# Low passes of the product with v, and tile 0's scores, threaded between the transposes of their slot

## The chip, the cores and the metric

The kernel runs on one core of a Trainium2 chip. The time is the device time of one execution in microseconds (us). TensorE (PE) multiplies; loading its weights is listed by itself as PEld. VectorE is DVE, ScalarE is ACT, GpSimd is POOL, and SP is the engine that issues most transfers. PSUM is the memory TensorE writes to; the kernel uses six banks of it in rotation (tag `b`) and two as accumulators.

## The reference

Attention with a forgetting gate, then a layer norm and a two-layer network with a residual:

```python
scores = scale * q @ k.T                        # 8 batches x 8 heads, 576 tokens, 64 wide
decay = cum[:, None] - cum[None, :]             # cum = cumsum(log(clip(f, 1e-4, 1)))
scores = where(causal, -1e9, scores + decay)
attn = softmax(scores);  x = attn @ v           # heads side by side: 8 x 576 x 512
xn = (x - mean) / sqrt(var + 1e-6) * g_ln
out = x + relu(xn @ w_ch1) @ w_ch2              # 512 -> 2048 -> 512
```

All values are f32. To multiply exactly enough at the faster fp32r rate, most operands are split into a high part (rounded to fp32r) and a low part (the residual), and a product is the sum of high x high, high x low and low x high passes.

## The kernel before

**Slots.** The 64 heads are cut into query tiles: tile 0 has the first 64 queries, tiles 1 to 4 have 128 each (`QT`, line 296). Tile t sees the keys up to its own: 64, 192, 320, 448 and 576. The loop at line 811 runs over slots (head, t) with t = 1 to 4; slot t = 1 also does tile 0. With `LAG` = 2, a slot computes the scores of its own tile, transposes the softmaxed tile of two slots ago, and, if the slot three ago was t = 2 or 4, does the product with v for that pair of tiles. So in the steady state of a head:

| slot | scores | product with v | transposes (64-column block, 128-column blocks) |
|---|---|---|---|
| t = 1 | tiles 0 and 1 | tiles 0 to 2 of the head before | tile 3 of the head before: 1, 3 |
| t = 2 | tile 2 | none | tile 4 of the head before: 1, 4 |
| t = 3 | tile 3 | tiles 3, 4 of the head before | tiles 0 and 1: 2, 1 |
| t = 4 | tile 4, in two halves | none | tile 2: 1, 2 |

Every slot from number 35 on also carries one step of the network (`mm1`, lines 624 to 626, 12 matmuls of 256 columns; `mm2`, lines 646 to 648, 6 matmuls of 512 columns of the step before). 64 such steps remain behind the last slot.

**Two kinds of head.** The first 16 heads (`NFULL`) multiply in f32 and have no low passes. The other 48 split their operands: scores are `hi` x `hi` (L377) plus `kl`, `xq` (L378); the product with v (`av_unit`, line 512) has high passes with both halves of v as 128-column weights (`both(k)`, moving `ph`) and low passes with the 64-column high half of v (moving `pl`). All write the bank `o`.

**A tile's way.** `softmax_a` (DVE L410) adds the mask and scales the scores and takes the row minimum of the negated values. `softmax_e` (ACT L421) takes the exponential with its row sum. `softmax_b` (DVE L426, L427, POOL L428) normalizes; a transfer (`pw<-p`, SP) copies the tile as fp32r. Two slots later `transpose_unit` (line 455) puts its blocks through TensorE into the bank `tr` (L447; L449 for f32). A block's weights are the 64 or 128 columns of the tile, its moving operand is the identity of 128 columns. `transposed_hi` (ACT L505) rounds `tr` to `ph`, and `transposed_lo` (DVE L510) writes the residuals: for the 64-key block into the lower half of `ph`, for the others into `pl`. So both kinds of pass read what DVE wrote. `finish` (ACT L580) copies the upper half of `o` to `ot`; `finish_add` (DVE L591) adds it to the lower half and gives `xs`, which is sent to memory.

**The order** in a slot is written out by hand in `ORDERS` (line 50): one letter a piece, one string for each stage. Every engine runs its own instructions in exactly that order.

```python
(66, "QSAFteahBlMPrmNbRLD"),
```

This third string holds from slot 66 to the last, number 258. Q is the scores, S `softmax_a`, A the product with v, F `finish`, t the transposes, e the exponential, a `finish_add`, h and l the two casts, B `softmax_b`, M `mm1`, P preparations of the next head (ACT L343, L349, DVE L350, L357), r and m the split of the hidden values (ACT L632, DVE L637), N `mm2` and, after a chunk's last step, the output (DVE L723), b the statistics of rows (ACT L687, DVE L692, L693), R loads and splits of the network's input (ACT L607, DVE L609), L and D small steps and loads. A bank is taken again once its last reader in this order is through; banks are handed out in the order in which they came free.

A chunk of the network has 256 tokens and 16 steps, so the work of N, b and R beyond the single step repeats every 16 slots, that is every four heads.

Of the kernel before, what the change touches and what calls it, by code (L numbers as in the profile page):

```python
# [17 lines left out]
P = 128  # L18
# [30 lines left out]

ORDERS = [  # L50
    (0, "WwQsSthAeMrgFBmlLNPaRf"),
    (37, "WwQSstAMhPelgNFrfmBDLRba"),
    (66, "QSAFteahBlMPrmNbRLD"),
]


# [1 line left out]
def attn_moe(ctx: ExitStack, tc: tile.TileContext, qk, v, f, g, w1, w2, out):  # L58
# [396 lines left out]
    def transpose_unit(h, t):  # L455
        n = f"{h.n}"
        pt = h.p[t][0]
        work_ = []
        if t <= 2:
            if t == 1:  # L460
                if h.full:
                    h.ph1 = padded_keys("ph1", 704, S1)
                else:
                    h.ph1 = work.tile([P, 704], F32R, tag="ph1", bufs=1, name=f"ph1_{n}")
                h.pl1 = None if h.full else pools["late"].tile([P, 384], F32R, tag="pl1", bufs=1, name=f"pl1_{n}")
            ph = h.ph1
            pl = ph if h.full else h.pl1
            tp = bank(f"tr{n}_{t}")
            if t == 1:
                tr(tp[0:64, 0:128], h.p[0][0])  # L470
                tr(tp[0:64, 64:192], pt[:, 0:64])
                tr(tp[:, 192:320], pt[:, 64:192])
                work_.append((tp[0:64, 0:192], ph[0:64, 0:192], ph[64:128, 0:192]))
                work_.append((tp[:, 192:320], ph[:, 320:448], pl[:, 0:128]))
            else:
                tr(tp[0:64, 0:128], pt[:, 0:64])
                tr(tp[:, 128:256], pt[:, 64:192])
                tr(tp[:, 256:384], pt[:, 192:320])
                work_.append((tp[0:64, 0:128], ph[0:64, 192:320], ph[64:128, 192:320]))
                work_.append((tp[:, 128:384], ph[:, 448:704], pl[:, 128:384]))  # L480
        else:
            if t == 3:
                if h.full:
                    h.ph2 = padded_keys("ph2", 9 * P, S - S1)
                else:
                    h.ph2 = work.tile([P, 9 * P], F32R, tag="ph2", bufs=1, name=f"ph2_{n}")
                h.pl2 = None if h.full else pools["late"].tile([P, 7 * P], F32R, tag="pl2", bufs=1, name=f"pl2_{n}")
            c = 0 if t == 3 else P
            ph = h.ph2[:, : 8 * P].rearrange("p (k c) -> p k c", k=4)[:, :, c : c + P]
            pl = None if h.full else h.pl2[:, : 6 * P].rearrange("p (k c) -> p k c", k=3)[:, :, c : c + P]  # L490
            tp = bank(f"tr{n}_{t}").rearrange("p (k c) -> p k c", k=4)
            tr(tp[0:64, 0, :], pt[:, 0:64])
            for k in range(1, 4):
                tr(tp[:, k, :], pt[:, 64 + P * (k - 1) : 64 + P * k])
            work_.append((tp[0:64, 0, :], ph[0:64, 0, :], ph[64:128, 0, :]))
            work_.append((tp[:, 1:4, :], ph[:, 1:4, :], pl))
            if t == 4:
                tp = bank(f"tr{n}_4b")[:, :P]
                tr(tp, pt[:, 64 + 3 * P : 64 + 4 * P])
                work_.append((tp, h.ph2[:, 8 * P :], None if h.full else h.pl2[:, 6 * P :]))  # L500
        h.parts = work_

    def transposed_hi(h, t):
        for tp, hi, lo in h.parts:
# [7 lines left out]
    def av_unit(h, t):  # L512
        po = bank(f"o{h.n}_{t}")

        if h.full:

            def fac(cols, k, mv, first=False):
                half = slice(0, 64) if cols.start < SPLIT[t] else slice(64, P)
                mm(po[half, cols], h.vr[:, k], mv, start=first, stop=True, skip_group_check=True)  # L519

            if t == 2:
                ph = h.ph1
                for k, c0, q0 in ((0, 0, 0), (1, 320, 64)):
# [12 lines left out]
            return  # L536

        vv = h.vv

        def both(k):  # L540
            return vv[:, k].rearrange("p a d -> p (a d)")

        def acc(o, st, mv, first=False):
            mm(o, st, mv, start=first, stop=True, skip_group_check=True)  # L544

        if t == 2:
            ph, pl, w, c0 = h.ph1, h.pl1, S1, 0
            acc(po[:, 0:320], both(0), ph[:, 0:320], True)
            acc(po[:, 64:320], both(1), ph[:, 320:576])
            acc(po[:, 192:320], both(2), ph[:, 576:704])  # L550
            acc(po[0:64, 64:320], vv[:, 1, 0, :], pl[:, 0:256])
            acc(po[0:64, 192:320], vv[:, 2, 0, :], pl[:, 256:384])
        else:
            ph, pl, w, c0 = h.ph2, h.pl2, S - S1, S1
            for k in range(4):
                acc(po[:, 0:256], both(k), ph[:, 256 * k : 256 * k + 256], k == 0)
# [4 lines left out]
        h.o = (po, w, c0)  # L561

    xs_tile = {}

# [246 lines left out]
    for u, slot in enumerate(slots):  # L811

        def before(k):
            return slots[u - k] if u >= k else None

        if slot is not None:
            n, t = slot
            h = hd[n]
        av = None
        if before(LAG + 1) is not None and before(LAG + 1)[1] in (2, 4):  # L820
            av = hd[before(LAG + 1)[0]]
        want = moe.can(wp.ready()) and u >= FIRST_MOE

        def piece(c):
            tu = before(LAG)
            if c == "t" and tu is not None:
                transpose_unit(hd[tu[0]], tu[1])
            elif c == "h" and tu is not None:
                transposed_hi(hd[tu[0]], tu[1])
            elif c == "l" and tu is not None:  # L830
                transposed_lo(hd[tu[0]])
            elif c == "Q" and slot is not None:
                if t == 1:
                    qk_mm(h, 0)
                qk_mm(h, t)
            elif c == "A" and av is not None:
                av_unit(av, before(LAG + 1)[1])
            elif c == "S" and slot is not None:
                if t == 1:
                    softmax_a(h, 0)  # L840
                softmax_a(h, t)
            elif c == "e" and slot is not None:
                if t == 1:
                    softmax_e(h, 0)
                softmax_e(h, t)
            elif c in FILL:
                wp.fill(FILL[c])
            elif c == "s":
                wp.sums()
                if u == LAG:  # L850
                    busy(WARM[2])
            elif c == "F" and av is not None:
                finish(av)
            elif c == "a" and av is not None:
                finish_add(av)
            elif c == "r" and want:
                moe.first_high()
            elif c == "R":
                moe.limit = min(NCHUNK, max(0, u - LAG - 1) // (4 * H) * S // C)
                moe.rest()  # L860
            elif c == "b":
                rows_stats(moe.cur)
            elif c == "L":
                run_later(RSTD)
            elif c == "M" and want:
                moe.first()
            elif c == "B" and slot is not None:
                if t == 1:
                    softmax_b(h, 0)
                softmax_b(h, t)  # L870
            elif c == "m" and want:
                moe.first_low()
            elif c == "W":
                due = 1 + min(u, W_CHANGE) / W_SLOTS + max(0, u - W_CHANGE) * W_TICKS
                while not wp.done() and wp.tick_no <= due:
                    wp.tick()
            elif c == "N":
                moe.second()
            elif c == "P":
                prep()  # L880
            elif c == "D":
                next_raw()
# [90 lines left out]
```

## Time and profile before

| | |
|---|---|
| median of 3 runs | 1208.62 us (1208.13 to 1209.88) |
| the profiled execution | 1208.3 us |
| its span, first to last instruction | 1206.5 us |
| granted TensorE clock, mean | 0.997 |
| TensorE busy, span from 0 to 105 us | 91.00 us |
| TensorE busy, 250 to 990 us | 739.71 of 740 us |
| VectorE busy, 250 to 990 us | 530.23 us |
| ScalarE busy, 250 to 990 us | 411.47 us |
| GpSimd busy, 250 to 990 us | 331.25 us |

The first third of the table is the device time; the rest comes from one profiled execution. A matmul's recorded time runs from its start to the end of its pass through the array, which overlaps with the passes behind it: what a pass costs is read from the distance of two starts, not from its duration. A weight load runs beside the pass before it. An instruction of DVE or ACT is likewise listed with its whole latency, and the next may start a little before it has ended. In brackets stands the idle time of the engine before an instruction, and what ended it.

### The profile page before, as it was taken

Reading aid. Unit: us, or ns where it says so; the run is one execution under the profiler, and the core shown is the slowest. Engines: PE = TensorE matmul, PEld = TensorE weight load, DVE = VectorE, ACT = ScalarE, POOL = GpSimd, SP = SyncE. Lnnn points to the kernel's source line nnn. Section 1 sums busy time; section 2 is a strip of 40 time slices with the busy share of each in tenths; the row PEclk is TensorE's granted clock in tenths of the full one; section 3 lists DMA queues with packets and bytes.
Section 4 is the critical chain, followed back from the end, with each engine's and each line's share of the span. In section 5 each row is a group of like instructions: output and inputs, shape, how many; then the busy total and the mean of one; then the engine's idle time right before and its main releaser. Section 6 shows DMA issues by size and latency. Waiting matters only on the chain.

```text
span 1206.5 us, 25720 instructions
## 1 busy us (share of the span) xinstructions
PE 1187.0 (98%) x8368; PEld 1066.3 (88%) x8368; DVE 752.9 (62%) x2658; ACT 619.4 (51%) x1936; POOL 456.6 (38%) x774
## 2 busy tenths in 40 slices
PE   8889999999999999999999999999999999999998
PEld 6667888999999999999999999999999999999997
DVE  6787684476767777777767676767676752122222
ACT  5887575555555555555555555555565532111111
POOL 3445345344545444453545453444454410000000
PEclk9999999999999999999999999999999999999999
DMA  6455442344444443434343434444343421111100
GB/s 193 133 166 169 131 135 82 99 134 131 134 133 130 132 140 125 138 130 144 130 145 120 144 124 128 137 125 147 123 140 127 120 87 40 32 36 40 32 28 26
DMA packets 127541, 139.00 MB, mean 115 GB/s; under 512 B 32432, under 2 KB 100016, under 8 KB 127408
## 3 DMA queue, kind: packets, MB, share of 16 engines
q1 hardware_dynamic: 127408, 137.36, 37.2%
q8 instruction: 67, 1.10, 0.4%
q14 instruction: 66, 0.54, 0.2%
HBM read 79.61 MB, written 19.17 MB: 82 GB/s over the span
## 4 chain that ended last, share of the span: by engine, by line
PE 91%; DVE 3%; ACT 2%; DMA 1%; issue 1%; POOL 0%; SPq 0%; DVEq 0%; POOLq 0%; ACTq 0%
PE h L624 12%; PE h L626 11%; PE h L625 11%; PE acc L646 11%; PE acc L647 11%; PE acc L648 11%; PE o L544 6%; PE tr L447 4%; PE s L377 3%; PE s L378 3%; PE s L375 2%; PE o L519 2%; PE tr L449 1%; DVE p L410 1%; PE pc L202 1%
## 5 line engine op out<-in xcount | busy, mean ns | idle before, releaser
L428 POOL TENSOR_SCALAR p<-p,st 64x64 f32<-64x64 f32 (+4 forms) x320 | 169.6, 531 | 497.5 <-ACT ph L505 246.7
L624 PE MATMUL h<-x,w1h 128*128 128x256 f32 x1152 | 341.7, 297 | 0.4 <-DVE st L410 0.4
L626 PE MATMUL h<-x,w1l 128*128 128x256 f32 x1152 | 326.2, 283 | 0.0
L625 PE MATMUL h<-x,w1h 128*128 128x256 f32 x1152 | 325.7, 283 | 0.0
L421 ACT ACTIVATE p<-p,st 64x64 f32<-64x64 f32 (+4 forms) x320 | 179.2, 560 | 210.1 <-DVE st L410 205.7
L637 DVE SCALAR_TENSOR_TENSOR hh<-h,hh 128x256 fp32r<-128x256 f32 x288 | 120.5, 418 | 186.5 <-ACT hh L632 184.1
L646 PE MATMUL acc<-w2h,hh 128*128 128x512 f32 x576 | 228.4, 397 | 0.0
L647 PE MATMUL acc<-w2l,hh 128*128 128x512 f32 x576 | 227.8, 395 | 0.0
L648 PE MATMUL acc<-w2h,hh 128*128 128x512 f32 x576 | 225.4, 391 | 0.0
L624 PEld LDWEIGHTS h<-x,w1h 128*128 128x128 f32 x1152 | 219.0, 190 | 5.3 <-issue 0.9
L625 PEld LDWEIGHTS h<-x,w1h 128*128 128x128 f32 x1152 | 220.0, 191 | 2.4
L626 PEld LDWEIGHTS h<-x,w1l 128*128 128x128 f32 x1152 | 219.7, 191 | 0.0
L632 ACT ACTIVATE hh<-h 128x256 fp32r<-128x256 f32 x288 | 109.9, 382 | 181.2 <-PE h L626 180.7
L410 DVE CUSTOM_DVE_ANT_0 p<-s,mask 64x64 f32<-64x64 f32 (+4 forms) x320 | 132.3, 421 | 26.2 <-PE s L378 17.4
L648 PEld LDWEIGHTS acc<-w2h,hh 128*128 128x128 f32 x576 | 108.5, 188 | 24.7
L426 DVE TENSOR_SCALAR st<-st 128x1 f32<-128x1 f32 (+1 forms) x320 | 47.7, 149 | 121.3 <-ACT p L421 118.2
L646 PEld LDWEIGHTS acc<-w2h,hh 128*128 128x128 f32 x576 | 109.4, 190 | 14.0 <-issue 0.2
L647 PEld LDWEIGHTS acc<-w2l,hh 128*128 128x128 f32 x576 | 109.4, 190 | 11.7
L505 ACT CAST ph<-tr 64x128 fp32r<-64x128 f32 (+4 forms) x384 | 107.2, 328 | 3.7 <-PE tr L447 1.3
L580 ACT COPY ot<-o 64x320 f32<-64x320 f32 x96 | 38.0, 396 | 124.1 <-PE tr L447 62.6
L510 DVE TENSOR_TENSOR pl<-tr,ph 128x128 fp32r<-128x128 f32 x192 | 88.0, 458 | 4.4
L378 PE MATMUL s<-kl,xq 66*128 66x288 f32 (+4 forms) x288 | 83.3, 297 | 0.0
(90 smaller groups left out, 1886.0 us busy)
## 6 DMA issues: line engine op xcount, KB each, us to landing
raw<-in_qk_dram SPq DMA_DIRECT2D x96, 288.0 KB
wr<-in_w_dram SPq DMA_DIRECT2D x32, 512.0 KB
pw<-p SPq DMA_DIRECT2D x48, 288.0 KB
pw<-p SPq DMA_DIRECT2D x48, 224.0 KB
vr<-in_v_dram SPq DMA_DIRECT2D x64, 160.0 KB
out_dram<-xt SPq DMA_DIRECT2D x36, 256.0 KB
pw<-p SPq DMA_DIRECT2D x48, 160.0 KB
xa<-xs SPq DMA_DIRECT2D x32, 160.0 KB
```

The costliest lines, as they stand in the source:

```text
L378: mm(sp, xq, kl, start=False, stop=True)
L410: nc.vector.tensor_tensor_reduce(out=pt[:m, a:z], in0=sp, in1=mask[:m, off + a : off + z], scale=-SCALE, scalar=3.0e38 if i == 0 else st[: ...
L421: nc.scalar.activation(pt[:m, :w], pt[:m, :w], AF.Exp, bias=st[:m, i : i + 1], scale=-1.0, accum_out=st[:m, 2:3])
L428: nc.gpsimd.tensor_scalar(out=pt[:m, :w], in0=pt[:m, :w], scalar1=st[:m, 3:4], scalar2=1.0, op0=ALU.mult, op1=ALU.mult)
L624: mm(ph, w1h[:, k, fs], c.x[k][:, 0, :], start=(k == 0), stop=False)
L625: mm(ph, w1h[:, k, fs], c.x[k][:, 1, :], start=False, stop=False)
L626: mm(ph, w1l[:, k, fs], c.x[k][:, 0, :], start=False, stop=(k == KT - 1))
L632: nc.scalar.activation(h[:, 0, :], c.ph, AF.Relu)
L637: nc.vector.scalar_tensor_tensor(out=h[:, 1, :], in0=ph, scalar=0.0, in1=h[:, 0, :].bitcast(F32), op0=ALU.max, op1=ALU.subtract)
L646: mm(c.acc[i], h[:, 0, ts_], w2h[:, j, :], start=(j == 0), stop=False)
L647: mm(c.acc[i], h[:, 0, ts_], w2l[:, j, :], start=False, stop=False)
L648: mm(c.acc[i], h[:, 1, ts_], w2h[:, j, :], start=False, stop=(j == FT - 1))
```

## The change

Four things move; no matmul, cast or transfer is added or taken away.

- In every group of transposes the 64-column blocks come last.
- The low passes of the product with v are no longer issued by `av_unit`; it returns them as a list, the shortest first. The piece t (`row`) issues them: one behind each wide transpose as long as another wide one follows and more than one low pass is left, the rest at the end of the row.
- Tile 0's scores (of the heads with split operands) leave Q and are issued in the row, behind the transposes and ahead of the remaining low passes. Their `softmax_a` and `softmax_e` are the new piece z.
- In the third string F moves from behind A to behind t and e, with z behind it; in the second, z comes behind l. In B tile 1 is normalized ahead of tile 0, in all heads.

```diff
-    (37, "WwQSstAMhPelgNFrfmBDLRba"),
-    (66, "QSAFteahBlMPrmNbRLD"),
+    (37, "WwQSstAMhPelzgNFrfmBDLRba"),
+    (66, "QSAteFzahBlMPrmNbRLD"),
...
             if t == 1:
+                tr(tp[:, 192:320], pt[:, 64:192])
                 tr(tp[0:64, 0:128], h.p[0][0])
                 tr(tp[0:64, 64:192], pt[:, 0:64])
-                tr(tp[:, 192:320], pt[:, 64:192])
...
-            acc(po[0:64, 64:320], vv[:, 1, 0, :], pl[:, 0:256])
-            acc(po[0:64, 192:320], vv[:, 2, 0, :], pl[:, 256:384])
+            low = [
+                lambda: acc(po[0:64, 192:320], vv[:, 2, 0, :], pl[:, 256:384]),
+                lambda: acc(po[0:64, 64:320], vv[:, 1, 0, :], pl[:, 0:256]),
+            ]
...
-            for k in range(1, 4):
-                acc(po[0:64, 0:256], vv[:, k, 0, :], pl[:, 256 * (k - 1) : 256 * k])
-            acc(po[0:64, 128:256], vv[:, 4, 0, :], pl[:, 6 * P :])
+            low = [
+                lambda: acc(po[0:64, 128:256], vv[:, 4, 0, :], pl[:, 6 * P :]),
+                lambda: acc(po[0:64, 0:256], vv[:, 1, 0, :], pl[:, 0:256]),
+                lambda: acc(po[0:64, 0:256], vv[:, 2, 0, :], pl[:, 256:512]),
+                lambda: acc(po[0:64, 0:256], vv[:, 3, 0, :], pl[:, 512:768]),
+            ]
...
+        def row():
+            tu = before(LAG)
+            trs = [] if tu is None else transpose_unit(hd[tu[0]], tu[1])
+            wide = [x for x in trs if x[1].shape[1] > 64]
+            narrow = [x for x in trs if x[1].shape[1] <= 64]
+            while wide:
+                tr(*wide.pop(0))
+                if wide and len(lows) > 1:
+                    lows.pop(0)()
+            for x in narrow:
+                tr(*x)
+            if slot is not None and t == 1 and not h.full:
+                qk_mm(h, 0)
+            while lows:
+                lows.pop(0)()
...
             elif c == "B" and slot is not None:
-                if t == 1:
-                    softmax_b(h, 0)
-                softmax_b(h, t)
+                for i in [1, 0] if t == 1 else [t]:
+                    softmax_b(h, i)
+            elif c == "z" and slot is not None and t == 1 and not h.full:
+                softmax_a(h, 0)
+                softmax_e(h, 0)
```

So the slot t = 1 issues on TensorE: tile 1's scores, three high passes, wide transpose, low pass of 128 columns, two wide transposes, the 64-column block, tile 0's scores, low pass of 256 columns. The slot t = 3: tile 3's scores, five high passes, the wide transpose, two 64-column blocks, four low passes.

More of the change, by code (lines that the diff above doesn't have):

```diff
@@ L457, in transpose_unit, with tr @@
         pt = h.p[t][0]
-        work_ = []
+        work_, row = [], []
+        def tr(out_, in_):
+            row.append((out_, in_))
         if t <= 2:
@@ L475, in transpose_unit @@
             else:
-                tr(tp[0:64, 0:128], pt[:, 0:64])
                 tr(tp[:, 128:256], pt[:, 64:192])
                 tr(tp[:, 256:384], pt[:, 192:320])
+                tr(tp[0:64, 0:128], pt[:, 0:64])
                 work_.append((tp[0:64, 0:128], ph[0:64, 192:320], ph[64:128, 192:320]))
@@ L491, in transpose_unit @@
             tp = bank(f"tr{n}_{t}").rearrange("p (k c) -> p k c", k=4)
-            tr(tp[0:64, 0, :], pt[:, 0:64])
             for k in range(1, 4):
@@ L497, in transpose_unit @@
             if t == 4:
-                tp = bank(f"tr{n}_4b")[:, :P]
-                tr(tp, pt[:, 64 + 3 * P : 64 + 4 * P])
-                work_.append((tp, h.ph2[:, 8 * P :], None if h.full else h.pl2[:, 6 * P :]))
+                tb = bank(f"tr{n}_4b")[:, :P]
+                tr(tb, pt[:, 64 + 3 * P : 64 + 4 * P])
+                work_.append((tb, h.ph2[:, 8 * P :], None if h.full else h.pl2[:, 6 * P :]))
+            tr(tp[0:64, 0, :], pt[:, 0:64])
         h.parts = work_
+        return row
     def transposed_hi(h, t):
@@ L535, in av_unit @@
                 h.o = (po, S - S1, S1)
-            return
+            return []
         vv = h.vv
@@ L557, in av_unit @@
             acc(po[:, 128:256], both(4), ph[:, 8 * P :])
-            for k in range(1, 4):
-                acc(po[0:64, 0:256], vv[:, k, 0, :], pl[:, 256 * (k - 1) : 256 * k])
-            acc(po[0:64, 128:256], vv[:, 4, 0, :], pl[:, 6 * P :])
+            low = [
[4 more added lines that the diff above has]
+            ]
         h.o = (po, w, c0)
+        return low
     xs_tile = {}
@@ L818, in attn_moe @@
             h = hd[n]
-        av = None
+        av, lows = None, []
         if before(LAG + 1) is not None and before(LAG + 1)[1] in (2, 4):
@@ L822, in attn_moe, with tiles @@
         want = moe.can(wp.ready()) and u >= FIRST_MOE
+        def tiles(h, t):
+            return [0, 1] if t == 1 and h.full else [t]
+        def row():
[13 more added lines that the diff above has]
+                lows.pop(0)()
         def piece(c):
             tu = before(LAG)
-            if c == "t" and tu is not None:
-                transpose_unit(hd[tu[0]], tu[1])
+            if c == "t":
+                row()
             elif c == "h" and tu is not None:
@@ L832, in piece @@
             elif c == "Q" and slot is not None:
-                if t == 1:
-                    qk_mm(h, 0)
-                qk_mm(h, t)
+                for i in tiles(h, t):
+                    qk_mm(h, i)
             elif c == "A" and av is not None:
-                av_unit(av, before(LAG + 1)[1])
+                lows.extend(av_unit(av, before(LAG + 1)[1]))
             elif c == "S" and slot is not None:
-                if t == 1:
-                    softmax_a(h, 0)
-                softmax_a(h, t)
+                for i in tiles(h, t):
+                    softmax_a(h, i)
             elif c == "e" and slot is not None:
-                if t == 1:
-                    softmax_e(h, 0)
-                softmax_e(h, t)
+                for i in tiles(h, t):
+                    softmax_e(h, i)
             elif c in FILL:
```

1 line of the change is left out of this document (removed).

## The prediction

> **What bounds the kernel now.** The page comes first: the busy table, then the chain that ended last.
>
> ```profile
> span 1206.5 us, 25720 instructions
> PE 1187.0 (98%) x8368; PEld 1066.3 (88%) x8368; DVE 752.9 (62%) x2658; ACT 619.4 (51%) x1936; POOL 456.6 (38%) x774
> PE 91%; DVE 3%; ACT 2%; DMA 1%; issue 1%; POOL 0%; SPq 0%; DVEq 0%; POOLq 0%; ACTq 0%
> ```
>
> TensorE is never idle for long and holds 91% of the chain, so a microsecond taken out of its stream is a microsecond, as long as nobody comes late to it. The stream has hidden losses, though. The timeline of PE shows one head (start, duration): its first slot, its third, and the start of the next head.
>
> ```profile
> 709.72 0.22 PE L377 MATMUL s<-hi 128*64 128x128 f32 x1
> 709.84 0.30 PE L377 MATMUL s<-hi 128*128 128x192 f32 x1
> ...
> 710.09 0.51 PE L544 MATMUL o<-ph,vv 128*128 128x320 f32 x3
> 710.44 0.34 PE L544 MATMUL o<-pl,vv 128*64 128x256 f32 x2
> 710.61 0.46 PE L447 MATMUL tr<-identr,pw 128*64 128x128 f32 x4
> 710.91 0.35 PE L624 MATMUL h<-x,w1h 128*128 128x256 f32 x1
> 711.10 0.28 PE L625 MATMUL h<-x,w1h 128*128 128x256 f32 x1
> ...
> 717.39 0.37 PE L377 MATMUL s<-hi 128*128 128x448 f32 x1
> ...
> 717.80 0.70 PE L544 MATMUL o<-ph,vv 128*128 128x256 f32 x5
> 718.34 0.57 PE L544 MATMUL o<-pl,vv 128*64 128x256 f32 x4
> 718.75 0.35 PE L447 MATMUL tr<-identr,pw 128*64 128x128 f32 x3
> 718.93 0.35 PE L624 MATMUL h<-x,w1h 128*128 128x256 f32 x1
> 719.12 0.28 PE L625 MATMUL h<-x,w1h 128*128 128x256 f32 x1
> ...
> 725.47 0.22 PE L377 MATMUL s<-hi 128*64 128x128 f32 x1
> ```
>
> Read the starts. Three transposes with 128 moving columns take 718.75 to 718.93, 0.06 each; the two tile-0 scores (709.72 to 709.84) also 0.06 each. A 256-column pass, the four low passes show it (718.34 to 718.75 for three of 256 and one of 128), takes 0.12. Yet L624 behind transposes takes 0.19 (710.91 to 711.10). The first slot: four transposes and L624 take 0.49, where 4 x 0.06 + 0.12 = 0.36 would do; 0.13 lost, with three 128-column transposes. The third slot: 0.37 against 0.30; 0.07 lost, with one. So each 128-column transpose whose weights load behind a 0.06 pass loses about 0.03, and a full load (128x128, not transposing) behind one about 0.04 to 0.05.
>
> The other side is VectorE and ScalarE, which the page calls 62% and 51% busy. Both take their instructions in the order written. Their timeline in the same head, with the end of the head before:
>
> ```profile
> 702.66 0.62 DVE L410 CUSTOM_DVE_ANT_0 p<-s,mask 128x448 f32<-128x448 f32 x1
> ...
> 706.60 0.44 DVE L410 CUSTOM_DVE_ANT_0 p<-s,mask 128x288 f32<-128x288 f32 x1
> ...
> 710.06 1.02 DVE L609 TENSOR_TENSOR x<-xr,x 128x256 fp32r<-128x256 f32 x2
> 711.00 0.21 DVE L410 CUSTOM_DVE_ANT_0 p<-s,mask 64x64 f32<-64x64 f32 x1
> ...
> 711.14 0.34 DVE L410 CUSTOM_DVE_ANT_0 p<-s,mask 128x192 f32<-128x192 f32 x1
> ...
> 711.42 0.47 DVE L591 TENSOR_TENSOR xs<-o,ot 64x320 f32<-64x320 f32 x1
> ...
> 712.82 0.28 DVE L510 TENSOR_TENSOR ph<-tr,ph 64x128 fp32r<-64x128 f32 x1 [0.31 <-ACT ph L505]
> ...
> 713.92 1.40 DVE L723 SCALAR_TENSOR_TENSOR xt<-acc,rs,xt 128x512 f32<-128x512 f32 x2
> 715.24 0.48 DVE L410 CUSTOM_DVE_ANT_0 p<-s,mask 128x320 f32<-128x320 f32 x1
> ...
> 716.97 0.28 DVE L510 TENSOR_TENSOR ph<-tr,ph 64x128 fp32r<-64x128 f32 x1 [0.17 <-ACT ph L505]
> ...
> 718.33 0.61 DVE L410 CUSTOM_DVE_ANT_0 p<-s,mask 128x448 f32<-128x448 f32 x1
> ...
> 719.41 0.42 DVE L591 TENSOR_TENSOR xs<-o,ot 64x256 f32<-64x256 f32 x1 [0.46 <-ACT ot L580]
> 720.07 0.16 DVE L426 TENSOR_SCALAR st<-st 128x1 f32<-128x1 f32 x1 [0.24 <-ACT p L421]
> ...
> 722.29 0.46 DVE L410 CUSTOM_DVE_ANT_0 p<-s,mask 128x288 f32<-128x288 f32 x1
> ...
> 725.10 0.42 DVE L510 TENSOR_TENSOR pl<-tr,ph 128x256 fp32r<-128x256 f32 x1
> ```
>
> ```profile
> 711.59 0.44 ACT L421 ACTIVATE p<-p,st 128x192 f32<-128x192 f32 x1
> ...
> 712.15 0.64 ACT L505 CAST ph<-tr 64x128 fp32r<-64x128 f32 x2
> ...
> 719.00 0.37 ACT L580 COPY ot<-o 64x256 f32<-64x256 f32 x1 [1.05 <-PE tr L447]
> 719.27 0.67 ACT L421 ACTIVATE p<-p,st 128x448 f32<-128x448 f32 x1
> ...
> 720.06 0.47 ACT L505 CAST ph<-tr 64x192 fp32r<-64x192 f32 x2
> ```
>
> VectorE is 62% busy and yet often behind: the 192-column scores stand ready soon after 710, and it reaches them at 711.14; each wait in it is a link of one chain through ScalarE and back. TensorE does not notice today, because what it needs from that chain (ph and pl, for the next product with v) comes in time: pl of 725.10 ends at 725.52, and the first low pass of the next head comes 0.72 behind its slot's start (709.72 to 710.44), at 726.19.
>
> **The change on TensorE.** Passes and columns stay the same; only neighbours change. Per head of the 48 that have low passes (64 heads less NFULL = 16): slots 2 and 4 end their row with a 64-column block in place of opening it; one 128-column load fewer stands behind a 0.06 pass, 0.03 each. Slot 3: the transposes come ahead of the low passes, so L624's load stands behind a 0.12 pass and is covered; of 0.07 the 0.03 of one transpose remain, 0.05 saved. Slot 1: tile 1's full load no longer stands behind tile 0 (0.05), L624's stands behind the 256-column low pass (0.05), and the wide transposes lose 0.03 three times as before: 0.10. Together 0.10 + 0.03 + 0.05 + 0.03 = 0.20 with unrounded shares 0.198, times 48: **9.5 us less**, if every operand is in time. A 64-column load behind a transpose has no row; between nothing and the 0.03 of a wide one, I take nothing (such loads hide behind 0.06 passes in the tile-0 scores). For two of them per head the other end is 48 x 2 x 0.03 = 2.9.
>
> A rule of the Trainium skill speaks against this term. The row first, PEld being the weight loads:
>
> ```profile
> 710.87 0.19 PEld L624 LDWEIGHTS h<-x,w1h 128*128 128x128 f32 x1
> ```
>
> This load starts at 710.87 while the transposes of 710.61 run until 711.07, on the same 128 rows. The Trainium skill, page "TensorE: Matmul & The Clock Gate", section "Part 3: Packing small matmuls — row/col tiling", says that a load overlaps running matmuls only where the row groups differ. By that rule no order hides a load, and the 9.5 would be 0; by the row it stands.
>
> The first 16 heads use f32 passes and have no low passes; there only the blocks and the normalizations of tiles 0 and 1 change places. The waits of PE say what hangs on it (who, on whom, us in total, times, longest):
>
> ```profile
> PE tr L449 <- POOL p L428: 3.7, 10, 0.7
> ```
>
> These transposes need both tiles before they end, and the second of GpSimd's two multiplications ends when it did, so I take nothing. At best the 3.7 goes; as much again could come, since tile 1's exponential is the later one.
>
> **The change on VectorE and ScalarE.** This decides. In the new order the copy of o (L580) stands behind the tile's exponential on ScalarE, and the addition L591, which reads the copy, still stands ahead of the normalization on VectorE. VectorE now waits for exponential and copy in a row, and the residuals ph, pl and the next slot's scores queue behind it.
>
> Slot 3, from the start of its scores to those of slot 4 when VectorE is late: before 718.33 to 722.29, 3.96. After: scores until the exponential 0.66 (0.61 and a short read), exponential with its read 0.79 (719.27 to 720.06), copy to addition 0.41 (719.00 to 719.41), addition 0.36, then 720.07 to 722.29 is 2.22, less 0.14 of waiting for the cast that ends at 720.53. Sum 4.30.
>
> Slot 1, likewise: before 711.00 to 713.92, 2.92. After: scores of tile 1 to the exponential 0.38, exponential 0.56 (711.59 to 712.15), copy 0.46, addition 0.40, four small steps of 0.17 0.69, residuals and hh 1.10 (712.82 to 713.92). Sum 3.59. Tile 0's scores and exponential fall into the waits.
>
> Slots 2 and 4 keep their 3.09 (715.24 to 718.33) and 3.50 (722.29 to 725.79, which is 725.10 plus the 0.69 to the next scores).
>
> Now replay. Let VectorE take 702.66 as before. The next scores start at 702.66 + 4.30 = 706.96 (before 706.60), and pl ends 3.23 later (722.29 to 725.52), at 710.19. TensorE, two heads ahead by 0.20 each, starts slot 1 at 709.32; its first low pass now comes 0.66 behind the slot's start (0.72 less tile 0's 0.12, plus one transpose), at 709.98, with 0.11 for signal and load: 710.30 against 709.98. **Wait 0.3.** VectorE is free at 710.42, does the two L609 in 0.68 (part of their 1.02 is waiting that a later start swallows; 0.68 is my choice between 0.6 and the 0.94 from 710.06 to 711.00), starts slot 1 at 711.10, slot 2 at 711.10 + 3.59 + 1.32 (both L723) = 716.01, and its ph ends 2.01 later at 718.02. TensorE reaches slot 3 at 717.39 - 0.40 - 0.13 (slots 1 and 2 of this head) + 0.3 = 717.16, and its product with v, 0.41 later, at 717.57 needs that ph. **Wait 0.5**, and 0.1 more at the low pass that now comes first. Slot 3's scores 719.10, slot 4's 723.40 (1.11 late); pl ends 726.63. TensorE's next head starts 725.47 - 0.60 + 0.3 + 0.6 = 725.77, its low pass stands at 726.43, needs 726.74. **Wait 0.3.** The following head has neither L609 nor L723 ahead of its first slots and catches up. Sum 1.2 a round. How many rounds, the grouped lines of VectorE over 250 to 990 tell:
>
> ```profile
> L723 DVE SCALAR_TENSOR_TENSOR xt<-acc,rs,xt 128x512 f32<-128x512 f32 x24 | 16.8, 742 | 0.0
> ```
>
> 24 are 12 pairs, one every fourth head: 12 x 1.2 = 14.6 with the unrounded 1.22. Sum: 1208.3 (the profiled execution's own time, its span and 1.8 around it) - 9.5 + 14.6 = 1213.4. The median of the three runs is 1208.62, 0.3 above that execution; **forecast 1213.7**.
>
> **Rivals.** (1) *Faster*: VectorE's idle time swallows the later addition. For it: the brackets above show 0.2 to 0.5 of idle several times a head. Against: each is a link of the chain that I counted. It decides if the waits of a round stay under 0.6 (0.79 saved, less 0.2). With 0.2 left a round: 1208.6 - 9.5 + 2.4 = 1201.5. Chance 0.22. (2) *No change*: the waits come only around the head with L723 (0.5 and 0.3), because the head before it is in time: 1208.6 - 9.5 + 9.6 = 1208.7. Chance 0.18. (3) *The change hides no load*: each pass pays its load in whatever order, so nothing is saved, and the waits stay: 1208.6 + 14.6 = 1223. The load that runs beside the transposes from 710.87 speaks against it. Chance 0.03. (This is what the rule cited from the Trainium skill would give.) (4) The forecast, 0.57.
>
> **How the numbers follow.** The two lengthened chains are good to some 0.15 each; three of them meet in a round, so 0.45 x 12 = 5.4 either way, 1208 to 1219. Above that, rounds whose L609 waits longer, and the DMA of pw that goes out later: 1221. Below, rival 1 reaches from 1199.1 with no waits; I cut at 1201, leaving out about 1 in 10 on each side. A measurement of this kernel tells 0.2% (2.4 us) from no change. Faster 0.22, same 0.18, slower 0.60.
>
> **What would show it.** Right: in the new trace, L624 behind the row in slots 1 and 3 takes 0.12; L591 stands idle for ACT L580 longer than now; PE L544 shows waits for DVE L510, in the heads with L723 and at the start of the next. Wrong: the scores of slot 4 start as close to TensorE as now, or the product with v never waits; then the 9.5 comes out whole. If L624 still takes 0.19, the TensorE side is wrong.

## The result and the profile after

The changed kernel takes **1230.05 us** (median of 4 runs, 1228.17 to 1232.64), the kernel before 1208.84 beside it: ratio 1.0175, 95% interval 1.0158 to 1.0192. It is slower, as forecast, but by 21 us and not by 5, and outside the range. The profiled execution has a span of 1226.4 us against 1206.5. One of the ten executions of a run below, the one without the output additions, took 2271 us, and its time there is the median of the other nine.

In the changed file most lines stand lower. The ones used here, old to new: ScalarE's cast to ph L505 to L510, VectorE's residual L510 to L515, the product with v L544 to L549, the copy of o L580 to L591, the addition L591 to L602, the chunk's cast and residual L607 and L609 to L618 and L620, the MLP's first pass L624 to L635, the output addition L723 to L734. Heads are told apart by n modulo 4, since one MLP chunk takes four heads: in n%4 = 1 the first two pieces of the chunk's input are split (L618, L620), in n%4 = 2 its row statistics are taken (L703), at the turn from n%4 = 2 to 3 the other two pieces are split, and in n%4 = 3 the output additions L734 follow. The head shown in the prediction, at 709.72, is n = 47, of the kind 3.

The page of the changed kernel:

```profile
span 1226.4 us, 25577 instructions
PE 1190.1 (97%) x8368; PEld 1062.9 (87%) x8368; DVE 745.1 (61%) x2658; ACT 626.3 (51%) x1936; POOL 454.8 (37%) x774
PE 21%; ACT 1%; issue 1%; DVE 1%; POOL 1%; DMA 0%; SPq 0%; DVEq 0%; POOLq 0%; ACTq 0%
```

No engine has more work than before, and TensorE still reads 97%. The chain of waits, 91% TensorE before, holds only a quarter of the span here: the view lost the trail, so nothing is read from it. The waits of PE say more (who, on whom, us in total, times, longest):

```profile
PE o L549 <- DVE ph L515: 12.3, 33, 0.6
PE tr L449 <- POOL p L428: 6.4, 12, 1.1
PE o L549 <- POOL rs L725: 3.0, 10, 0.3
PE tr L447 <- DMA pw<-p: 1.0, 2, 0.8
```

The product with v now waits for the residuals of ph; before, that was one wait of 0.3. But the rows give 15 us where more than 20 are missing. The timeline of PE in head 47 shows why (its first slot, its third, and the start of its fourth):

```profile
719.81 0.25 PE L377 MATMUL s<-hi 128*128 128x192 f32 x1
719.90 0.28 PE L378 MATMUL s<-kl,xq 66*128 66x192 f32 x1
720.50 0.57 PE L549 MATMUL o<-ph,vv 128*128 128x320 f32 x3 [0.32 <-POOL rs L725]
720.90 0.24 PE L447 MATMUL tr<-identr,pw 128*128 128x128 f32 x1
...
721.42 0.28 PE L549 MATMUL o<-pl,vv 128*64 128x256 f32 x1
721.54 0.28 PE L635 MATMUL h<-x,w1h 128*128 128x256 f32 x1
721.65 0.28 PE L636 MATMUL h<-x,w1h 128*128 128x256 f32 x1
...
727.91 0.37 PE L377 MATMUL s<-hi 128*128 128x448 f32 x1
728.11 0.36 PE L378 MATMUL s<-kl,xq 66*128 66x448 f32 x1
728.97 0.80 PE L549 MATMUL o<-ph,vv 128*128 128x256 f32 x5 [0.50 <-DVE ph L515]
729.61 0.37 PE L447 MATMUL tr<-identr,pw 128*128 128x128 f32 x3
729.81 0.58 PE L549 MATMUL o<-pl,vv 128*64 128x128 f32 x4
730.23 0.28 PE L635 MATMUL h<-x,w1h 128*128 128x256 f32 x1
730.35 0.28 PE L636 MATMUL h<-x,w1h 128*128 128x256 f32 x1
...
733.06 0.30 PE L377 MATMUL s<-hi 128*128 128x288 f32 x1
```

First, the saving is there: L636 follows L635 by 0.11 and 0.12 in both slots, where the kernel before took 0.19. Second, the waits are larger than their brackets. From 719.90 to 720.50 there are 0.60 between two starts that otherwise lie 0.11 apart, so 0.49 are lost, and the bracket says 0.32: the record of the pass before runs on to 720.18 and covers the first part of the wait. The Trainium skill, page "Perfetto Trace Analysis", section "Tensor Engine Instruction (MATMUL, LD_WEIGHTS)", says that the end which the profile gives a TensorE instruction is computed, not observed; the rows here agree. Waits of this engine are therefore read from start to start.

So read, slot by slot (start of a slot's first full score to the next slot's; medians over the 12 heads of a kind, in us; "copy early" and the others are runs of the next section):

| slot | before | changed | load early | no output addition | copy early | copy and load early |
|---|---|---|---|---|---|---|
| 1, n%4 = 0 | 3.97 | **4.41** | 4.40 | 4.01 | 4.01 | 4.02 |
| 1, n%4 = 2 | 4.26 | **4.83** | 4.30 | 4.91 | 4.30 | 4.30 |
| 1, n%4 = 3 | 3.97 | **4.55** | 4.45 | 4.52 | 4.01 | 4.01 |
| 3, n%4 = 3 | 4.44 | **5.13** | 5.12 | 4.40 | 4.59 | 4.60 |

Without a wait the four slots of a head take 3.97 + 3.58 + 4.44 + 3.76 = 15.75 before and 4.01 + 3.54 + 4.40 + 3.62 = 15.56 (unrounded) in the changed kernel (tile 0's 0.12 has moved from in front of slot 1 into it). That is 0.19 less; unrounded and with the longer slots of n%4 = 1 and 2 it comes to 9.4 us over 48 heads. Against it, the four places lose 0.41, 0.53, 0.54 and 0.73 in each round of four heads, 2.21, times 12 rounds 26.5 us; the waits in all other slots come to 5.6, against 2.8 before. 26.5 + 2.8 - 9.4 = 19.9, and the span grew by 19.9.

Where the waits come from, on VectorE (its timeline, heads 46 to 47):

```profile
713.17 0.62 DVE L410 CUSTOM_DVE_ANT_0 p<-s,mask 128x448 f32<-128x448 f32 x1
...
715.03 0.42 DVE L602 TENSOR_TENSOR xs<-o,ot 64x256 f32<-64x256 f32 x1 [1.22 <-ACT ot L591]
...
717.59 0.44 DVE L410 CUSTOM_DVE_ANT_0 p<-s,mask 128x288 f32<-128x288 f32 x1
...
720.06 0.28 DVE L515 TENSOR_TENSOR ph<-tr,ph 64x128 fp32r<-64x128 f32 x1
...
722.00 0.34 DVE L410 CUSTOM_DVE_ANT_0 p<-s,mask 128x192 f32<-128x192 f32 x1
...
723.42 0.48 DVE L602 TENSOR_TENSOR xs<-o,ot 64x320 f32<-64x320 f32 x1 [0.92 <-ACT ot L591]
...
724.43 0.28 DVE L515 TENSOR_TENSOR ph<-tr,ph 64x128 fp32r<-64x128 f32 x1
...
725.53 1.40 DVE L734 SCALAR_TENSOR_TENSOR xt<-acc,rs,xt 128x512 f32<-128x512 f32 x2
...
728.63 0.28 DVE L515 TENSOR_TENSOR ph<-tr,ph 64x128 fp32r<-64x128 f32 x1 [0.17 <-ACT ph L510]
...
729.99 0.61 DVE L410 CUSTOM_DVE_ANT_0 p<-s,mask 128x448 f32<-128x448 f32 x1
...
734.26 0.44 DVE L410 CUSTOM_DVE_ANT_0 p<-s,mask 128x288 f32<-128x288 f32 x1
```

Slot 3 now takes VectorE 4.42 (713.17 to 717.59) and 4.27 (729.99 to 734.26); slot 1 up to L734 takes 3.53 (722.00 to 725.53). The addition stands 0.4 to 1.0 idle for the copy in every slot 1 and 1.2 in nearly every slot 3; the residual of 728.63 ends at 728.91, and the product follows at 728.97. Grouped over 250 to 990 us, before and then changed (busy, mean ns of one, idle ahead and what ended it):

```profile
L580 ACT COPY ot<-o 64x256 f32<-64x256 f32 x93 | 36.8, 395 | 122.1 <-PE tr L447 62.6 <-PE o L544 59.4
L591 DVE TENSOR_TENSOR xs<-o,ot 64x256 f32<-64x256 f32 x93 | 41.7, 448 | 32.6 <-ACT ot L580 32.1
L607 ACT CAST x<-xr 128x256 fp32r<-128x256 f32 x46 | 17.4, 405 | 14.3 <-DMA xr<-xb 7.5 <-DMA xr<-xa 6.8
```

```profile
L591 ACT COPY ot<-o 64x320 f32<-64x320 f32 x91 | 36.0, 396 | 2.2
L602 DVE TENSOR_TENSOR xs<-o,ot 64x320 f32<-64x320 f32 x91 | 41.0, 451 | 89.5 <-ACT ot L591 89.5
L618 ACT CAST x<-xr 128x256 fp32r<-128x256 f32 x46 | 17.4, 405 | 19.6 <-DMA xr<-xa 11.2 <-DMA xr<-xb 8.5
```

Before, the copy lay in 122 us of idle time of ScalarE; now it stands right behind the exponential, with casts behind it, and the addition waits 57 us more. The last row is one that the prediction didn't use: ScalarE's cast of the chunk's input waits for its load.

### The profile page after: what moved, and what is told of

Its sections match the earlier page's. It is cut to its first block, busy times and chain, and to the rows that moved or that the text cites. A ratio compares the mean times of both kernels' runs of the same rounds, so it can differ in the third digit from the quotient of the medians.

```text
span 1226.4 us, 25577 instructions
## 1 busy us (share of the span) xinstructions
PE 1190.1 (97%) x8368; PEld 1062.9 (87%) x8368; DVE 745.1 (61%) x2658; ACT 626.3 (51%) x1936; POOL 454.8 (37%) x774
## 5 line engine op out<-in xcount | busy, mean ns | idle before, releaser
L428 POOL TENSOR_SCALAR p<-p,st 128x192 f32<-128x192 f32 (+4 forms) x320 | 169.5, 535 | 514.4 <-ACT ph L510 213.6
L635 PE MATMUL h<-x,w1h 128*128 128x256 f32 x1152 | 334.0, 290 | 0.5 <-DVE st L410 0.4
L636 PE MATMUL h<-x,w1h 128*128 128x256 f32 x1152 | 325.1, 282 | 0.0
L635 PEld LDWEIGHTS h<-x,w1h 128*128 128x128 f32 x1152 | 218.7, 190 | 5.7 <-issue 0.9
L636 PEld LDWEIGHTS h<-x,w1h 128*128 128x128 f32 x1152 | 219.2, 190 | 2.5
L510 ACT CAST ph<-tr 64x128 fp32r<-64x128 f32 (+4 forms) x384 | 107.4, 328 | 3.7 <-PE tr L447 1.4
L602 DVE TENSOR_TENSOR xs<-o,ot 64x320 f32<-64x320 f32 x96 | 43.3, 451 | 95.2 <-ACT ot L591 95.2
L515 DVE TENSOR_TENSOR pl<-tr,ph 128x128 fp32r<-128x128 f32 x192 | 88.0, 458 | 4.4
L447 PE MATMUL tr<-identr,pw 128*128 128x128 f32 (+1 forms) x672 | 86.5, 234 | 1.4 <-DMA pw<-p 1.0
```

What stands on the lines that cost most here:

```text
L428: nc.gpsimd.tensor_scalar(out=pt[:m, :w], in0=pt[:m, :w], scalar1=st[:m, 3:4], scalar2=1.0, op0=ALU.mult, op1=ALU.mult)
L510: nc.scalar.copy(out=hi, in_=tp)
L635: mm(ph, w1h[:, k, fs], c.x[k][:, 0, :], start=(k == 0), stop=False)
L636: mm(ph, w1h[:, k, fs], c.x[k][:, 1, :], start=False, stop=False)
```

## The experiments

All ratios are against runs of the kernel before on the same chip, with 95% intervals. In the piece strings F is the copy, e the exponential, z tile 0's late reads and exponential, a the addition, h and l casts and residuals of ph, t the row of transposes.

**1. The copy's place.** Four orders.

```
-    (66, "QSAteFzahBlMPrmNbRLD"),      (the changed kernel)
+    (66, "QSAtFezahBlMPrmNbRLD"),      (copy early)
```

> The changed kernel with one edit: ScalarE's copy of o (L591) goes ahead of the exponential of its slot, as it does in the kernel before; the threaded rows and the late tile 0 stay. Theory A (the loss is VectorE's and ScalarE's order: the copy behind the exponential makes the addition, and the residuals behind it, late, and TensorE waits for them; the 9.5 us saved on TensorE are whole): the waits of PE for the residuals fall back to about the 4 us of before, and the time is 1201 to 1205 us (1208.8 less 9.5, plus 2 to 6, since the low passes now end 0.1 to 0.2 us later in their slot and the copy waits for them). Rival B (the threading or the late tile 0 delays VectorE wherever the copy stands): 1222 to 1232 us, the waits as in the changed kernel.

Measured 1207.11 us, ratio 0.9991 (0.9978 to 1.0004): one letter moved by one place takes 23 us back. The waits for ph fall from 12.3 to 1.8, and the table above shows three of the four places free. But it isn't the 1201 to 1205 expected: of the 9 us saved on TensorE about 1 comes out.

```
-    (66, "QSAFteahBlMPrmNbRLD"),       (the kernel before)
+    (66, "QSAteFahBlMPrmNbRLD"),       (copy late alone)
```

> The kernel before with one edit: the copy of o goes behind the exponential; no threading, no late tile 0. Theory A: VectorE's chain grows as in the changed kernel, and TensorE, 0.2 us a head slower than there, waits less by as much: waits of 2.26 us a round less 0.79, times 12, gives 17.6, so about 1226 us (1222 to 1230). If the waits were only those that the prediction counted (1.2 a round less 0.8): 1214. Rival B (the copy's place is harmless): 1207 to 1211 us.

Measured 1231.27 us, ratio 1.0177 (1.0160 to 1.0194): the copy's place, with nothing of the rest, costs as much as the whole change. That is 1 us above the expected 1222 to 1230: the slower TensorE did not wait less by what it is slower. Its slots show the same four places (slot 3 of n%4 = 3: 5.17 us against 4.44; slot 1 of n%4 = 0, 2 and 3: 4.09, 4.49 and 4.20 against 3.97, 4.26 and 3.97) and two more (slot 2 of n%4 = 2 and 3: 3.91 and 3.81 against 3.64 and 3.58). Between the starts of heads 20 and 60 a round of four heads takes 65.7 us here, 65.4 in the changed kernel and 63.8 before: of the 0.8 a round that the change saves on TensorE, 0.3 comes out as long as the copy is late.

```
-    (66, "QSAteFzahBlMPrmNbRLD"),      (the changed kernel)
+    (66, "QSAteFzhBlaMPrmNbRLD"),      (addition last)
```

> The changed kernel with one edit: VectorE's addition to xs (L602) goes behind the residuals of its slot; the copy stays behind the exponential. If the addition standing ahead of the residuals is what makes these late: the waits for ph and pl shrink, 1210 to 1220 us. If it is the copy itself, because ScalarE's cast of ph stands behind it and the residuals need that cast: the residuals come at the same time as now (0.66 scores + 0.79 exponential + 0.41 copy + 0.47 cast = 2.33 us behind the scores, against 2.38 in the changed kernel by way of the addition), and the addition only moves 0.4 us of work behind them: 1229 to 1235 us.

Measured 1285.87 us, ratio 1.0625 (1.0606 to 1.0645). The second reading was right in kind and its size far off. VectorE in a first slot of this run:

```profile
566.76 0.35 DVE L410 CUSTOM_DVE_ANT_0 p<-s,mask 128x192 f32<-128x192 f32 x1
...
569.30 0.28 DVE L515 TENSOR_TENSOR ph<-tr,ph 64x128 fp32r<-64x128 f32 x1 [0.32 <-ACT ph L510]
569.60 0.56 DVE L515 TENSOR_TENSOR pl<-tr,ph 128x384 fp32r<-128x384 f32 x1
570.19 0.48 DVE L602 TENSOR_TENSOR xs<-o,ot 64x320 f32<-64x320 f32 x1
```

The residual comes 2.54 behind the scores, hardly later than in the changed kernel (722.00 to 724.43, 2.43): it waits for the cast, and the cast stands behind the copy. The addition, in the changed kernel inside that idle time, now adds its 0.42 and 0.48 to every head. I expected 0.1 a slot, but the addition is only a part of it. Behind it in slot 3 stands L350, which casts the next head's q. Here it is in this run, beside an instruction of GpSimd, and then in the changed kernel:

```profile
577.36 1.43 POOL L351 TENSOR_TENSOR hi<-raw,hi 64x576 fp32r<-64x576 f32 x1 [0.42 <-POOL p L428]
577.82 1.29 DVE L350 CAST xq<-raw 64x576 fp32r<-64x576 f32 x1
```

```profile
733.11 0.51 DVE L350 CAST xq<-raw 64x576 fp32r<-64x576 f32 x1
733.39 1.51 POOL L351 TENSOR_TENSOR hi<-raw,hi 64x576 fp32r<-64x576 f32 x1
```

In the changed kernel the cast starts 0.28 ahead of GpSimd's L351 and takes 0.51. Pushed back by the addition it starts 0.2 to 0.5 behind the start of L351, and in all 45 heads from 250 us on it ends 0.31 to 0.32 behind L351's end: 1.40 us on average. 0.89 a head is 43 us over 48 heads, most of the 56 by which this run is slower than the changed kernel. VectorE's slot 3 takes 5.4 us in place of 4.3 to 4.4, and of this 1.0 to 1.1 the cast makes 0.8 to 1.0. With that, TensorE waits in heads of all four kinds (17.1 to 18.2 us each, 15.6 to 15.9 without waits). No run moves L351 by itself.

```
-    (66, "QSAteFzahBlMPrmNbRLD"),      (the changed kernel)
+    (66, "QSAtezhFBlaMPrmNbRLD"),      (copy behind the cast)
```

> The changed kernel with the copy of o behind the casts of ph and the addition behind the residuals, so that exponential, cast and residuals stand ahead of both. Theory A: the residuals come about 0.66 + 0.79 + 0.47 + 0.05 = 1.97 us behind the scores where before they came 2.25 behind, and slot 3 takes about 4.04 us where it took 3.96 before: few waits, 1199 to 1204 us. Rival B (threading or the late tile 0 is at fault): 1222 to 1232 us.

Measured 1211.11 us, ratio 1.0014 (1.0001 to 1.0028). With exponential and cast both ahead of the copy most of the loss is gone too, so it is the chain exponential, copy, cast, residual that made it, and not the late copy as such. But the expected 1199 to 1204 was missed: the time is some 11 us above what TensorE's saving would give, 3 more than with the copy early. Waits are left in slot 3 of n%4 = 3 (4.89 against 4.40) and in slot 1 of n%4 = 2 (4.43 against 4.30).

**2. Where TensorE's saving goes.** The parts alone, the copy early in each. Threading alone (tile 0 back in front):

```
-            return [0, 1] if t == 1 and h.full else [t]
+            return [0, 1] if t == 1 else [t]
...
+    (66, "QSAtFeahBlMPrmNbRLD"),
```

> The changed kernel with tile 0's scores, reads, exponential and normalization back in front of tile 1's, and the copy of o ahead of the exponential: of the change, the threaded low passes and the 64-key blocks last are left. TensorE saves about 0.15 us a head (0.198 less tile 0's 0.05), 7 us in all. If VectorE's chain has no slack, so that any saving comes back as waits for ph, pl and pw: 1204 to 1208 us. If the threading itself makes the copy and the addition late (the low passes end 0.1 to 0.2 us later in the slot): waits of 5 to 8 us, and 1207 to 1212. If the late tile 0 was the cost in the run with the copy early: 1201 to 1203, better than that run's 1207.

Tile 0 late alone:

```
+                for low in av_unit(av, before(LAG + 1)[1]):
+                    low()
...
+            for x in narrow + wide:
+                tr(*x)
...
+    (66, "QSAFtezahBlMPrmNbRLD"),
```

> The changed kernel with the low passes back right behind the high ones, the 64-key blocks first, and the copy ahead of the exponential: of the change, only the late tile 0 is left. TensorE saves about 0.05 us a head, 2.4 us in all. If the late tile 0 is harmless: 1206 to 1209 us. If tile 0's scores and exponential behind tile 1's lengthen slot 1 on VectorE and ScalarE: 1211 to 1216 us, with waits of the product with v in slots 1 and 3.

64-key blocks last alone (low passes right behind the high ones, tile 0 in front, the strings of the kernel before, among them `QSAFteahBlMPrmNbRLD`):

> The kernel before with one edit: the 64-key block of each row is transposed last. VectorE's and ScalarE's order is that of before. TensorE saves 0.03 us in each slot, about 0.1 us a head, 5 us in all. If a saving on TensorE is kept as long as the other engines' order is untouched: 1203 to 1205 us. If VectorE's chain has no slack, half or more of it comes back as waits: 1206 to 1209 us.

And copy early with the addition left out:

```
-            nc.scalar.copy(out=tmp[js, :w], in_=po[64:128, :w])
+            nc.scalar.copy(out=xs[js, :], in_=po[64:128, :w])
...
-            nc.vector.tensor_tensor(out=xs[js, :], in0=po[0:64, :w], in1=h.tmp[js, :w], op=ALU.add)
```

> The changed kernel with the copy of o ahead of the exponential, and with VectorE's addition of the two halves (L602) left out: the copy writes the upper half straight to xs. If VectorE's chain, now 0.8 us a head shorter, is what eats TensorE's saving: the waits for ph and pl go, and the time is 1198 to 1201 us (1208.8 less 9.5). If the saving was not there, or the waits come from transfers of pw or from TensorE itself: 1205 to 1208 us as with the addition.

| run | us | ratio (95%) | slots of a head without waits |
|---|---|---|---|
| threading alone | 1206.74 | 0.9986 (0.9969 to 1.0002) | 0.12 less |
| tile 0 late alone | 1208.18 | 0.9999 (0.9989 to 1.0009) | 0.05 less |
| 64-key blocks last alone | 1205.96 | 0.9973 (0.9962 to 0.9985) | 0.09 less |
| copy early, no addition | 1206.41 | 0.9974 (0.9963 to 0.9985) | 0.17 less |

The 64-key blocks keep the most: 0.086 times 48 is 4.1 us, and 3.3 come out. Threading saves 0.12 and keeps 1.7 of 5.8; the late tile 0 saves 0.05, 2.4 in all, and nothing of it can be told from noise. The last row is a miss: without the addition VectorE has 0.8 us a head less to do, and the time stays near 1207. So VectorE's load eats about 2 of the some 8 us that don't come out. With the copy early, 5.2 us of waits are left in slot 3 of the heads n%4 = 1 and slots 1 and 2 of n%4 = 2. In the head n%4 = 1 ScalarE does this (copy early; ScalarE's timeline, then SP's queue of the same head):

```profile
740.73 0.38 ACT L643 ACTIVATE hh<-h 128x256 fp32r<-128x256 f32 x1
742.89 0.41 ACT L618 CAST x<-xr 128x256 fp32r<-128x256 f32 x1 [1.77 <-DMA xr<-xb]
```

```profile
738.05 0.47 SPq L441 DMA_DIRECT2D pw<-p  x1
738.57 1.48 SPq L333 DMA_DIRECT2D vr<-in_v_dram  x1
740.10 0.43 SPq L671 DMA_DIRECT2D xr<-xa  x1
740.57 0.43 SPq L671 DMA_DIRECT2D xr<-xb  x1
```

The load of xr is issued behind the transfer of pw, which waits for the normalization, and in this head behind an issue of vr that took 1.48 us. ScalarE stands 1.77 us for it. VectorE's residual of the piece (L620) stands 1.27 for ScalarE's cast; behind it come VectorE's next scores, and behind these the next exponential.

**3. The load of xr one slot earlier**, its splits where they were:

```
-                if n >= self.limit or left > 8:
+                if n >= self.limit or left > 9:
...
-            old = len(c.xr)
+            old, c.seen = len(c.xr) if left == 0 else c.seen, len(c.xr)
```

> The changed kernel with the copy of o ahead of the exponential (as in the run that took 1207.1 us), and the four loads of each MLP chunk (xr) one slot earlier, with their splits (ScalarE's cast, VectorE's L620) in the slots where they are now. That run saved 9.5 us on TensorE and lost 7.6 to new waits; leaving out the addition did not bring them back. Theory C (in the head with the chunk's splits ScalarE's cast waits 0.8 to 2 us for the load of xr, and the copy, the exponential and the casts of ph queue behind it; before, the slack of the round swallowed this): the cast's waits on DMA go from 20 us to under 5, the waits of PE for ph shrink, 1201 to 1204 us. Rival D (the waits come from the transfers of pw or from late tile 0): 1206 to 1208.

> The kernel before with the 64-key blocks last (the run that took 1206.0 us) and the loads of xr one slot earlier. That version had hardly any wait of TensorE left, so under either theory the earlier load gives it little: 1203 to 1206 us. If the waits for xr cost more than PE's rows show: 1200 to 1203.

> The kernel before with the loads of xr one slot earlier, as a control. Theory C: ScalarE's waits for xr go, but TensorE did not wait behind them here, so 1207 to 1210 us. If the wait for xr costs time whatever the order: 1203 to 1206.

> The threaded rows alone (tile 0 in front, copy early: the run that took 1206.7 us) with the loads of xr one slot earlier. Its saving on TensorE is about 7 us, of which 2 came out. Theory C: 1202 to 1204 us. Rival D (its waits are those of the transposes of slot 2 for the transfer of pw, up to 0.9 us long in the profile): 1206 to 1208.

| load early, with | us | ratio (95%) | the same without the early load |
|---|---|---|---|
| copy early | 1203.37 | 0.9951 (0.9939 to 0.9964) | 0.9991 |
| 64-key blocks last alone | 1204.44 | 0.9960 (0.9947 to 0.9973) | 0.9973 |
| the kernel before | 1207.77 | 0.9990 (0.9976 to 1.0004) | 1 |
| threading alone | 1202.76 | 0.9950 (0.9933 to 0.9968) | 0.9986 |

ScalarE's wait for the load, copy early without and with the early load (250 to 990 us):

```profile
L618 ACT CAST x<-xr 128x256 fp32r<-128x256 f32 x46 | 17.4, 406 | 16.9 <-DMA xr<-xa 9.2 <-DMA xr<-xb 7.8
```

```profile
L618 ACT CAST x<-xr 128x256 fp32r<-128x256 f32 x46 | 17.3, 403 | 0.0
```

The control tells it: the early load does nothing measurable for the kernel before, and gives 4 to 5 us to copy early and to threading alone, where TensorE is faster. The wait had been there all the time, and the kernel before lost next to nothing by it. With the copy early, the 5.2 us of waits in the three slots named fall to 1.1 with the early load. The early load also takes these issues out of SP's queue ahead of that slot's transfers of pw, whose four waits of TensorE (1.3 us) go too; how much of the gain comes by that way was not separated. Copy early with early load and threading with early load are the two best versions found, 6 us faster than the kernel before. Of 9 us saved the first keeps 6; 2.4 of the rest is slot 3 of n%4 = 3 (4.60 against 4.40, times 12). Neither threading alone (4.39) nor the late tile 0 alone (4.44, as before) has that wait, so it takes both.

**4. What made the changed kernel's waits twice as large as forecast.** The changed kernel, once with the early load, once without the output additions:

> The changed kernel, copy of o behind the exponential and all, with the loads of xr one slot earlier. The waits of TensorE in the changed kernel come to 28 us, 15 were forecast. By the trace they fall in four places of a round of four heads: slot 1 of the head n%4 = 0 (5.3), of 2 (6.9) and of 3 (5.3), and slot 3 of 3 (8.6). If ScalarE's wait for xr, in the head before n%4 = 2, is what the forecast left out: the 6.9 go and the 5.3 of the next head shrink, 1219 to 1224 us. If VectorE's longer chain alone makes them: 1227 to 1231.

```
-            nc.vector.scalar_tensor_tensor(out=xt, in0=c.acc[i], scalar=c.rs[:, i : i + 1], in1=xt, op0=ALU.mult, op1=ALU.add)
```

> The changed kernel with VectorE's two 128x512 additions of the chunk's output (L734) left out; the output is then x without the MLP's part. The forecast put half of its waits (the 0.5 and 0.1 of slot 3, the 0.3 behind) down to these 1.4 us standing ahead of the next slots. If so: the waits in slot 3 of the head n%4 = 3 (8.6 us) and in slot 1 of the next (5.3) go, the other two stay, 1214 to 1219 us. If the additions only fill time in which VectorE would stand anyway: 1226 to 1230.

Measured 1223.58 us, ratio 1.0115 (1.0088 to 1.0142), and 1215.47 us, ratio 1.0054 (1.0038 to 1.0071). Each takes away its own places and leaves the others, as the columns of the first table show. Of the second run's gain 3.3 us fall behind the last head's scores, where the output additions are left out too (from there to the end 226.2 us in place of 229.5). PE in slot 1 of head 46 (n%4 = 2) with the early load, and in slot 3 of head 47 without the additions:

```profile
704.01 0.28 PE L378 MATMUL s<-kl,xq 66*128 66x192 f32 x1
704.12 0.51 PE L549 MATMUL o<-ph,vv 128*128 128x320 f32 x3
```

```profile
721.45 0.37 PE L378 MATMUL s<-kl,xq 66*128 66x448 f32 x1
721.66 0.70 PE L549 MATMUL o<-ph,vv 128*128 128x256 f32 x5
```

Both products follow their scores at the usual 0.11 and 0.21. One part of the expectation of the early load failed: the wait in the next head's slot 1 (n%4 = 3) did not shrink much (4.45 against 4.55 by medians). Most of it belongs to the longer chain.

## Why the prediction was right in direction and wrong in size

- **TensorE's saving.** Forecast 0.198 a head; the slots without waits give 0.19. Shown, also by the 64-key blocks alone, where nothing but their place on TensorE changes and 3.3 us come out. This refutes the third rival, that no order hides a load, though its 1223 lay nearer to the result than the forecast. The Trainium skill's rule cited there (page "TensorE: Matmul & The Clock Gate", section "Part 3: Packing small matmuls — row/col tiling") does not hold for these passes if it is taken alone; the same section also lets a load go ahead into a background weight buffer, which no run here shows or excludes.
- **The longer chain.** Forecast 4.30 for slot 3 and 3.59 for slot 1; measured 4.42 and 4.27, and 3.53. Right, and its cause too: moving the copy alone, forth or back, makes or removes the loss.
- **The step that failed is the replay of the waits**, 1.22 a round, where the trace shows 2.21 in the four places. First, it began with "Let VectorE take 702.66 as before", in the middle of the head n%4 = 2. The wait that had by then happened in this head's slot 1, 0.53 a round and 6.4 us in all, was left out. Its source, ScalarE waiting for the chunk's load in the head before, is a row of the kernel before (L607, 14.3 us idle); the early load takes this place away, and 6.5 us with it. The replay followed VectorE and TensorE and treated ScalarE as always on time. Second, the three waits that it did count came to 0.41, 0.54 and 0.73 instead of 0.3, 0.3 and 0.6: 0.46 a round, 5.5 us. Some of that is slot 3's chain, 0.1 longer before head 47; some is the restart of TensorE, put at 0.11 from no row and measured below at 0.16 to 0.20; and in slot 1 the replay let TensorE wait for pl at its low pass, where the trace shows the first high pass waiting for the residual in ph, which needs to be there earlier (720.06 + 0.28 against a start at 720.01 without a wait). How the 5.5 divide between these was not measured.
- **The part that belongs to L723** was put in the right places (slot 3 of head 47, slot 1 of the next): without the additions both waits go.
- **The rivals.** With the idle time of VectorE swallowing the later addition (rival 1) the product wouldn't wait; it waits in every round. Rival 2 kept only the waits around L723; the others are there too. The range ended at 1221, because its bounds varied the three counted waits and held none for an uncounted one.
- **The first 16 heads** were taken as nothing. GpSimd's row grew from 3.7 to 6.4, yet the first full score of head 16 starts at 213.64 in place of 213.39. That is right within what can be told: in the other runs with the same order up to there it starts at 212.7 to 214.0.
- **What hung on "if every operand is in time"** for the 9.5 was a larger condition than I took it for: with the copy back in its place, 1 us of 9 came out until the load of xr was moved too.

## What to carry to other kernels

An instruction moved by one place on an in-order engine costs what stands behind it, not its own duration: the copy takes 0.4 us, and behind the exponential it moved every cast and residual of its slot. When the bounding engine gets faster, look next for waits of other engines that its losses have covered; here they were rows of the old profile (an idle time in front of an instruction, ended by a DMA). A replay has to run a whole period with every engine in it, from a state that the replay itself produces. And an instruction moved in time also meets others than before: the cast L350 in the run with the addition last.

## What the runs showed of the hardware beyond that

- **One wait or two.** In the changed kernel the product with v starts 0.055 us behind the end of ph's residual in slot 3, and 0.146 behind it in slot 1, within 0.002 in all 45 late starts. In slot 3 the instruction waits on one semaphore, in slot 1 on two (VectorE's and, for vv, GpSimd's, long since given); there the trace lists the wait for VectorE as an instruction of its own in PE's sequencer, 0.05 us long, ahead of the weight load. In head 47: 728.63 + 0.28 to 728.97, and 720.06 + 0.28 to 720.50. With the pass after it 0.05 (slot 1) and 0.10 (slot 3) later than where nothing was late (0.22 against 0.17 and 0.12, medians), a late operand costs TensorE 0.20 and 0.16 from its end on. That the second semaphore makes the difference wasn't tried by itself.
- **A releaser by accident.** The row "POOL rs L725: 3.0, 10" names small operations of GpSimd that happened to end 0.03 ahead of the product in the heads n%4 = 3; in the other heads, with the same 0.146 behind the residual, GpSimd had ended its last operation 1.3 to 1.6 us earlier. The releaser there is VectorE's residual.
- **A cast that ends with another engine's instruction.** VectorE's L350 takes 0.44 us before and 0.51 in the changed kernel where it starts ahead of GpSimd's L351, and 1.3 or 1.5 us where it starts behind it (addition last), always ending 0.31 to 0.32 behind L351's end. The addition L602 beside the same L351 (577.37) took 0.42, as elsewhere. What holds the cast is not shown.
- **An issue that takes longer.** With the copy early, SP's issue of vr at 738.57 took 1.48 us, against 0.58 for the same issue in the kernel before; the loads of xr behind it started that much later. What held it stays open.
